# A recurrent layer and a feed-forward layer in one kernel: six weight tensors fetched ahead, the first products by token blocks, idle products in the front

## The chip, the cores and the metric

The kernel runs on one core of a Trainium2 chip. The metric is the device time of one execution in microseconds (us). The engines are named as the profile names them: PE is TensorE (matrix products; PEld is its loading of weights), DVE is VectorE, ACT is ScalarE, POOL is GpSimd, and SP is SyncE, which here only issues DMAs.

## The reference

Two layers follow each other. The first is a recurrence over 768 tokens in 4 batches of 8 heads, of head size 40; its output y, as 3072 rows of 320, goes through two matrix products with a softplus between them.

```python
    for t in range(S):
        kt, vt, qt = (k[:, :, t], v[:, :, t], q[:, :, t])
        m_new = np.maximum(f_gate[:, :, t] + m, i_gate[:, :, t])
        f_stab = np.exp(f_gate[:, :, t] + m - m_new)
        i_stab = np.exp(i_gate[:, :, t] - m_new)
        m = m_new
        C = f_stab[:, :, None, None] * C + i_stab[:, :, None, None] * np.einsum('bhd,bhe->bhde', vt, kt)
        n = f_stab[:, :, None] * n + i_stab[:, :, None] * kt
        h_tilde = np.einsum('bhde,bhe->bhd', C, qt)
        nq = np.einsum('bhd,bhd->bh', n, qt)[:, :, None]
        denom = np.maximum(np.abs(nq), 1.0)
        o = 1.0 / (1.0 + np.exp(-o_gate[:, :, t]))
        y[:, :, t] = o * h_tilde / denom
...
    h = x @ w_in
    g = np.maximum(h, 0.0) + np.log1p(np.exp(-np.abs(h)))
    return (g @ w_out).astype(np.float32)
```

Here x is y as 3072 rows of 320, w_in is 320 x 2048 and w_out 2048 x 320.

## The kernel before

The recurrence is computed in chunks of 128 tokens: 4 batches of 6 chunks are 24 steps, and three steps make one of 8 blocks of 384 tokens. Inside a chunk the recurrence becomes scores (sp), decays (pw) and products of the two with the values (yp). A tile x of 128 tokens by 320 is y, transposed on PE (xp) and cast by ACT into the high part of X; DVE subtracts to get its low part. X is what the second layer reads.

The second layer has 16 slices f of 128 of the 2048 hidden columns. For each block and slice PE makes hp from X with 8 products of 384 columns (wih and wil are the high and low parts of w_in, which the first engine mode needs to keep the precision), ACT makes the softplus gh, and PE adds gh times w_out to three banks po, one for each 128 tokens. In block 0 these last products use wof, the whole w_out in full precision; in later blocks its high and low parts woh and wol. The tiles hp lie in three buffers of PSUM (the tag hp), so a fourth slice waits until ACT has read the first.

The weights come as 16 tensors of 640 KB, wi0 to wi7 and wo0 to wo7, each holding two slices. They arrive as 64-bit words, and ACT (mag and sg, L218 to L233), POOL (some of the sg, L227) and DVE (L236) make 32-bit numbers of them in four instructions; then ACT casts the high parts (L260, L264 and L281) and DVE or POOL subtracts the low ones (L269, L271). Three of the raw tensors fit in the buffers at once (WB). This work, the next block's recurrence and the products run together through block 0.

The order of the instructions on each engine is fixed by in_order(): each follows the one written before it. What is written when is decided by tables. In the front, up to the first hp, the table F gives each event a number and the events run in the order of these numbers (in first_tile). Then products() counts the products of PE, and tick(n) runs every generator whose due count, from the tables Q, W, M, N, CI and CO, has been reached. Odd or even numbers of some entries of Q choose the engine (G: the conversion sg on POOL or ACT; H and J: the low parts on POOL or DVE).

Where ACT needs a function from another table of functions than the one loaded, a table load (ACT_TABLE_LOAD) stands in its order. In the front these are the sigmoids of the gates og and eg, the exponentials, and the softplus of gh.

later_gates() computes the gates of all chunks but the first: it reads the gate rows, takes exponentials, and scans; the results fz and fc go out to memory and come back spread over partitions (fb, fc).

Of the kernel before, what the change touches and what calls it, by code (L numbers as in the profile page):

```python
# [8 lines left out]
F32 = mybir.dt.float32  # L9
F32R = mybir.dt.float32r  # L10
# [34 lines left out]
def mlstm_moe_kernel(  # L45
# [113 lines left out]
    def later_gates():  # L159
# [3 lines left out]
        fs = p1.tile([NCHAIN, S], F32, tag="gb", name="fs")  # L163
        fg = fs[:, L:]
# [11 lines left out]
        nc.scalar.copy(fs[:, 0:L], fg0)  # L176
# [3 lines left out]
        fc = p1.tile([NCHAIN, S], F32, tag="gc", name="fc")  # L180
# [6 lines left out]
        nc.vector.tensor_tensor_scan(fc, fs, fc, 0.0, ALU.mult, ALU.add)  # L187
# [18 lines left out]
    woh = cpool.tile([128, NF, DM], F32R, name="woh")  # L206
# [67 lines left out]

    def weights_out(u, slope=False):
# [5 lines left out]
        nc.scalar.copy(woh[:, 2 * u : 2 * u + 2, :], wof[u])  # L281
# [13 lines left out]
    M = dict(FB=-23, LOAD=-50, Y=-9, SCAN=3, VI=-10, VW=10, IQ=25, SP=27, SPD=12, CN=33, CD=43, CE=49, CF=50, YQ=54,  # L295
             YQD=3, EV=47, YD=69, YD1=-30, RD=79, RY=-95, RZ=26, NM=116, FIN=128, XH=-9, XL=15)
    N = dict(FB=-26, LOAD=-57, Y=-7, SCAN=9, VI=-16, VW=22, IQ=23, SP=28, SPD=8, CN=30, CD=34, CE=39, CF=60, YQ=55,
             YQD=6, EV=17, YD=67, YD1=-32, RD=84, RY=-22, RZ=10, NM=125, FIN=150, XH=-9, XL=14)
    Q = dict(Gi0=68, Go0=50, Gi1=-42, Go1=1, Gi2=-47, Go2=36, Gi3=38, Go3=7, Gi4=6, Go4=18, Gi5=-8, Go5=31, Gi6=-10,
             Go6=7, Gi7=4, Go7=35, B3=40, B4=84, B5=125, B6=260, B7=300, B8=368, B9=446, B10=528, S0=-375, S1=-292,  # L300
             S2=-195, GT=-381, GL=52, LB=214, LS=33, SPD=-12, OF0=1, OF1=19, GR0=25, GR1=82, GR2=29, GR3=-26, GR4=18,
             GR5=38, LG=10, FS0=-51, FS1=25, FSW=-14, CI=-48, CO=-4, CS=34, K0=-23, K1=-29, CF=15, RC=-17, RS=92,
             B2=-20, B11=620, GT2=92, GL2=108, FS2=-31, GR6=-1, Hi0=-20, Ji0=63, Hi1=34, Ji1=78, Hi2=16, Ji2=34,
             Hi3=-12, Ji3=49, Hi4=-8, Ji4=-16, Hi5=36, Ji5=136, Hi6=-16, Ji6=107, Hi7=-67, Ji7=20)
    CI = dict(A=-6, B=2, C=-54, D=-2, E=10, F=30)
    CO = dict(A=3, B=-52, C=15, D=12, E=-36)
# [393 lines left out]
    def split_x(z):  # L700
# [3 lines left out]
        xp = work(z, ps_a, "pa", [128, 3, L], "xp", ps_h, "hp")  # L704
# [5 lines left out]
        nc.vector.tensor_tensor(X[:, 3:6, ts], xp, X[:, 0:3, ts], op=ALU.subtract)  # L710

# [3 lines left out]
    def first_tile(follow):  # L715
# [36 lines left out]
        for z in zs:  # L752
# [8 lines left out]
            fetch=fetch_next, fetch2=fetch_next, fetch3=fetch_next, wr=lambda: run(wparts),  # L761
        )
        for i, z in enumerate(follow):
            ev[f"lq{i}"] = lambda z=z: load(z)
            if i < 2:
                ev[f"lo{i}"] = lambda z=z: load_old(z)
# [154 lines left out]

    def products():
# [4 lines left out]
        def outs(po, t, f, put):  # L927
# [11 lines left out]
            else:  # L939
                terms = [(gh, woh[:, f]), (gh, wol[u][:, i]), (gl, woh[:, f])]  # L940
# [16 lines left out]
        for t in range(NT):  # L957
            po = []
            for f in range(NF):
                fsl = slice(f * 128, (f + 1) * 128)  # L960
                hp = ps_h.tile([128, T], F32, tag="hp", name=f"hp{t}_{f}")[:, 0 : SIZES[t] * L]
# [3 lines left out]
                X = Xs[t][:, :, 0 : SIZES[t] * L]  # L965
                seq = [
# [116 lines left out]
```

## Time and profile before

| | us |
|---|---|
| median of 3 runs | 462.56 |
| lowest and highest | 462.15, 462.60 |
| the profiled execution | 461.91 |
| its span on the chip | 460.2 |
| PE busy in the span | 433.4 |
| DVE, ACT, POOL busy | 303.9, 211.2, 137.2 |

The span is what the trace shows from the first instruction to the last; times below count from its start. The front lasts until the first hp product at 40.34, block 0 until about 105, and the blocks 1 to 7 fill the rest. The profile has a page with the busy time of the engines and other views: tables of busy time by stretch (with the granted clock of PE, where 1.00 is 2.4 GHz and 0.50 is 1.2 GHz), lists of what an engine waited for, and timelines of one engine, in which neighbouring instructions of one kind are one line. In a timeline a number in square brackets is the idle time before the line and who ended it.

### The profile page before, as it was taken

What the parts mean: (1) busy time and instruction counts of PE and PEld (TensorE: products, weight loads), DVE (VectorE), ACT (ScalarE), POOL (GpSimd) and SP (SyncE); (2) the same over time, 40 slices, a digit from 0 to 9 for tenths busy, and PEclk for the clock granted to TensorE, in tenths of its full rate; (3) what the DMA queues carried; (4) which work ended last, traced back from release to release, by engine and by line L of the source; (5) the groups of instructions that cost most, each with busy time, mean ns of one, the idle gap of its engine ahead of it and who ended that gap; (6) DMA issues with size and microseconds to landing.
All of it is one profiled execution on the core that took longest, in us unless ns stands there. A gap on an engine that the chain in (4) does not pass through costs nothing.

```text
span 460.2 us, 10555 instructions
## 1 busy us (share of the span) xinstructions
PE 433.4 (94%) x4266; PEld 402.9 (88%) x4266; DVE 303.9 (66%) x577; ACT 211.2 (46%) x416; POOL 137.2 (30%) x152
## 2 busy tenths in 40 slices
PE   5756799899999999999999999999999999999997
PEld 4555587677999999999999999999999999999996
DVE  4657488998987967766776867656876678242121
ACT  2727778784233642355333733463333543333332
POOL 8646078455531131233122312302223111000000
PEclk9975999999999999999999999999999999999999
DMA  7954967587656564654464263555374220101001
GB/s 200 333 188 115 274 197 246 147 214 168 178 180 182 154 151 122 164 144 96 150 185 117 74 204 108 129 143 138 105 196 129 78 78 19 41 0 46 0 1 43
DMA packets 38139, 62.55 MB, mean 136 GB/s; under 512 B 5626, under 2 KB 20258, under 8 KB 38090
## 3 DMA queue, kind: packets, MB, share of 16 engines
q1 hardware_dynamic: 25958, 53.62, 41.3%
q10 hardware_dynamic: 12132, 8.26, 6.3%
q8 instruction: 33, 0.54, 0.5%
q14 instruction: 16, 0.13, 0.1%
HBM read 53.60 MB, written 8.26 MB: 134 GB/s over the span
## 4 chain that ended last, share of the span: by engine, by line
PE 81%; DVE 9%; ACT 3%; POOL 3%; issue 2%; DMA 0%; SPq 0%; POOLq 0%; DVEq 0%; ACTq 0%
PE hp L978 36%; PE po L949 34%; PE yq L642 4%; PE sp L606 2%; PE sp L600 2%; POOL v L564 1%; DVE wof L236 1%; PE yp L619 1%; PE wm L723 1%; DVE wih L271 1%; PE fb L455 1%; DVE wil L269 1%; DVE mv L611 1%; DVE nm L685 1%; DVE gw L494 1%
## 5 line engine op out<-in xcount | busy, mean ns | idle before, releaser
L978 PE MATMUL hp<-X,wih 128*128 128x384 f32 x768 | 181.7, 344 | 4.0 <-ACT X L708 2.8
L978 PEld LDWEIGHTS hp<-X,wih 128*128 128x128 f32 x768 | 133.9, 189 | 9.0 <-ACT X L708 3.2
L854 ACT ACTIVATE gh<-hp 128x384 fp32r<-128x384 f32 x112 | 55.0, 491 | 181.8 <-PE hp L978 175.0
L858 DVE TENSOR_TENSOR gl<-hp,gh 128x384 fp32r<-128x384 f32 x112 | 61.6, 555 | 74.0 <-ACT hp L855 73.1
L949 PE MATMUL po<-wol,gh 128*128 128x320 f32 x336 | 71.2, 311 | 0.0
L949 PE MATMUL po<-woh,gl 128*128 128x320 f32 x336 | 70.3, 309 | 0.0
L949 PE MATMUL po<-woh,gh 128*128 128x320 f32 x336 | 69.8, 308 | 0.0
L978 PE MATMUL hp<-X,wil 128*128 128x384 f32 x256 | 66.6, 339 | 0.1
L500 POOL TENSOR_TENSOR vw<-vt,gw 128x328 f32<-128x328 f32 x23 | 21.7, 944 | 134.3 <-DVE gw L491 123.0
L564 POOL TENSOR_TENSOR v<-v,flast 40x328 f32<-40x328 f32 x37 | 38.2, 1032 | 69.4 <-DVE v L567 53.7
L949 PEld LDWEIGHTS po<-woh,gh 128*128 128x128 f32 x336 | 57.3, 188 | 0.1
L949 PEld LDWEIGHTS po<-woh,gl 128*128 128x128 f32 x336 | 54.9, 188 | 0.2
L949 PEld LDWEIGHTS po<-wol,gh 128*128 128x128 f32 x336 | 54.5, 188 | 0.5
L855 ACT ACTIVATE hp<-hp 128x384 f32<-128x384 f32 x112 | 54.5, 487 | 0.0
L978 PEld LDWEIGHTS hp<-X,wil 128*128 128x128 f32 x256 | 46.4, 189 | 0.9 <-DVE wil L269 0.5
L611 DVE TENSOR_TENSOR mv<-sp,pw 64x256 f32<-64x256 f32 x84 | 31.8, 417 | 14.7 <-PE sp L606 14.2
L482 POOL TENSOR_TENSOR v<-vt,gT 64x328 f32<-64x328 f32 x42 | 33.6, 801 | 22.5 <-DMA vt<-in_vko 19.6
L381 DVE TENSOR_TENSOR mv<-mv,fc 64x512 f32<-64x512 f32 (+1 forms) x42 | 39.1, 930 | 1.1 <-DMA fc<-fc_d 0.5
L949 PE MATMUL po<-wof,gh 128*128 128x320 f32 x96 | 28.5, 440 | 3.9 <-ACT v L544 2.7
L567 DVE TENSOR_TENSOR v<-v,sp 40x164 f32<-40x164 f32 x74 | 23.9, 323 | 12.0 <-POOL v L564 10.7
L439 DVE TENSOR_TENSOR_SCAN pw<-fb,near 128x512 f32<-128x512 f32 x21 | 26.4, 1255 | 3.8 <-DMA fb<-fz_d 3.8
L949 PEld LDWEIGHTS po<-wof,gh 128*128 128x128 f32 x96 | 17.6, 189 | 10.8 <-ACT v L544 3.0
(126 smaller groups left out, 439.9 us busy)
## 6 DMA issues: line engine op xcount, KB each, us to landing
qk<-in_qk SPq DMA_DIRECT2D x21, 416.0 KB
vt<-in_vko SPq DMA_DIRECT2D x23, 324.0 KB
fb<-fz_d SPq DMA_DIRECT2D x42, 128.0 KB
wi<-in_wts SPq DMA_DIRECT2D x8, 640.0 KB
wo<-in_wts SPq DMA_DIRECT2D x8, 640.0 KB
eg<-in_oT SPq DMA_DIRECT2D x7, 576.0 KB
out<-ob SPq DMA_DIRECT2D x24, 160.0 KB
yd<-y ACTq DMA_DIRECT2D x36, 96.0 KB
```

The costliest lines, as they stand in the source:

```text
L381: nc.vector.tensor_tensor(z.mv[ch][r], z.mv[ch][r], z.fc[r], op=ALU.mult)
L439: nc.vector.tensor_tensor_scan(pw.rearrange(flat), fb.rearrange(flat), eye.rearrange(flat), 0.0, ALU.mult, ALU.add)
L482: nc.gpsimd.tensor_tensor(vi, v1[r], g[r], op=ALU.mult)
L500: nc.gpsimd.tensor_tensor(z.vw, v1, z.gw.broadcast_to([128, H, E]), op=ALU.mult)
L564: nc.gpsimd.tensor_tensor(heads(whole), old, f, op=ALU.mult)
L567: nc.vector.tensor_tensor(dst[i], dst[i], z.cps[ch][dims(i)], op=ALU.add)
L611: nc.vector.tensor_tensor(half(z.mv[ch][r], i), sps[i][r], half(z.pw[r], i), op=ALU.mult)
L854: nc.scalar.activation(gh, hp, AF.Softplus)
L855: nc.scalar.activation(hp, hp, AF.Softplus)
L858: nc.vector.tensor_tensor(gl, hp, gh, op=ALU.subtract)
L949: nc.tensor.matmul(po[j], a[:, j * 128 : (j + 1) * 128], w, start=first, stop=(last and left[j] == 0))
L978: nc.tensor.matmul(hp, a, r, start=(i == 0), stop=(i == len(seq) - 1))
```

## The change

- Six weight tensors are loaded ahead. There are four raw buffers in place of three, and the fourth and fifth tensor (wi2 and wo1) go into buffers that will hold high parts of w_out later: woh, one tile before, becomes four tiles woh0 to woh3, and the two loads take the places of woh3 and woh2. On SP the five loads wi0, wi1, wo0, wi2, wo1 now stand in a row, and eg, qk and mv behind them.
- The eight products of the slices 0 and 1 of block 0 are made for each token block of 128 by itself, in the order blocks 1, 0, 2: 48 products of 128 columns in place of 16 of 384. They are events of the front now (h00 to h12), all behind the transposes and ahead of the third slice.
- keep_warm() puts products of the identity with itself, whose result wz nobody reads, into the front: 3 ahead of the first scores, 5 ahead of the second yp and 11 ahead of the last two xp.
- The tiles xp lie in the PSUM banks of po0, po1 and pa, not in those of hp.
- later_gates() holds the later gates apart from the first chunk's, without the copy of these (L176), scans in two parts and sends fz in two DMAs.
- The tables M, Q, CI, CO and F have new numbers. By them the third tile's scores go behind the first yp, the softplus table is loaded ahead of the eg sigmoids (o1s), the lows of wih of the tensors 2, 5 and 7 go from DVE to POOL, wil of 7 from POOL to DVE, and the conversions sg of wi6 and wo4 from ACT to POOL.

```diff
-        fs = p1.tile([NCHAIN, S], F32, tag="gb", name="fs")
-        fg = fs[:, L:]
+        fg = p1.tile([NCHAIN, w], F32, tag="gb", name="fg")
...
-        nc.scalar.copy(fs[:, 0:L], fg0)
...
-        nc.vector.tensor_copy(fc[:, 0:S:C], fs[:, 0:S:C])
-        nc.vector.memset(fs[:, 0:S:C], 0.0)
-        nc.sync.dma_start(fz_d.rearrange("c p s -> p c s"), fs.rearrange("p (c s) -> p c s", s=C))
+        parts = ((0, L, fg0), (L, S, fg))
+        for x, y, f in parts:
+            nc.vector.tensor_copy(fc[:, x:y:C], f[:, 0 : y - x : C])
+            nc.vector.memset(f[:, 0 : y - x : C], 0.0)
+            nc.sync.dma_start(fz_d[x // C : y // C].rearrange("c p s -> p c s"), f.rearrange("p (c s) -> p c s", s=C))
...
-    woh = cpool.tile([128, NF, DM], F32R, name="woh")
+    woh = [None] * (NF // 4)
...
-    WB, MB = 3, 2
+    WB, MB = 4, 2
+    STASH = (3, 4)
+    stashed = []
...
-        r = stage.tile([128, UW] + [2] * words, U32, tag="wr", bufs=WB, name=f"w{'io'[i]}{u}")
+        if words and len(raw) in STASH:
+            k = STASH.index(len(raw))
+            r = p1.tile([128, UW, 2], U32, tag=f"woh{3 - k}", name=f"w{'io'[i]}{u}")
+            stashed.append((6 - 2 * k, "io"[i] + str(u)))
+        else:
+            r = stage.tile([128, UW] + [2] * words, U32, tag="wr", bufs=WB, name=f"w{'io'[i]}{u}")
...
-        nc.scalar.copy(woh[:, 2 * u : 2 * u + 2, :], wof[u])
+        need(*[n for k, n in stashed if u >= k])
+        if u % 2 == 0:
+            woh[u // 2] = p1.tile([128, 4, DM], F32R, tag=f"woh{u // 2}", name=f"woh{u // 2}")
+        nc.scalar.copy(high(u), wof[u])
...
-    CI = dict(A=-6, B=2, C=-54, D=-2, E=10, F=30)
-    CO = dict(A=3, B=-52, C=15, D=12, E=-36)
+    CI = dict(A=-2, B=3, C=-81, D=9, E=0, F=30)
+    CO = dict(A=3, B=-76, C=15, D=8, E=-37)
...
-        xp = work(z, ps_a, "pa", [128, 3, L], "xp", ps_h, "hp")
+        xp = work(z, ps_a, "pa", [128, 3, L], "xp", *((ps_o, "po0"), (ps_o, "po1"), (ps_a, "pa"))[z.s])
...
+        def keep_warm(k):
+            n = max(0, Q[f"D{k}"])
+            if n and not idle:
+                idle.append(ps_h.tile([128, 4, 128], F32, tag="hp", name="wz"))
+            for i in range(n):
+                nc.tensor.matmul(idle[0][:, i % 4], ident, ident, start=True, stop=True)
...
+    def begin(f, g):
+        if f not in early:
+            early[f] = ps_h.tile([128, T], F32, tag="hp", name=f"hp0_{f}")
+        need(("X", g))
+        for _ in first_layer(early[f], 0, f, slice(g * L, (g + 1) * L)):
+            pass
...
-        zs = first_tile(rest[:3])
+        zs = first_tile(rest[:2])
```

first_layer() holds the eight products that stood in products(), for any range of tokens.

Three places show how the order moves. On PE, in the front: sp_0 are the scores of the third tile, sp_2 those of the second, yp_0_271 before and yp_0_267 after are the first attention product (the last numbers are the program's buffer numbers). Before:

```order
L585 MATMUL sp_0_0_261<-qk_0_144 128x128
L585 MATMUL sp_0_0_262<-qk_0_144 128x128
L619 MATMUL yp_0_271<-vi_0_221,pw_0_0_179 128x123 x4
L619 MATMUL yp_0_271<-vi_0_221,pw_0_1_181 128x123 x2
L619 MATMUL yp_0_271<-vi_0_221,pw_0_1_181 128x82
L619 MATMUL yp_0_271<-vi_0_221,pw_0_1_181 128x41
L619 MATMUL yp_0_288<-vi_0_233,pw_0_0_171 128x123 x4
```

After:

```order
L601 MATMUL sp_2_0_238<-qk_0_148 128x128
L601 MATMUL sp_2_0_239<-qk_0_148 128x128
L635 MATMUL yp_0_267<-vi_0_231,pw_0_0_168 128x123 x4
L635 MATMUL yp_0_267<-vi_0_231,pw_0_1_170 128x123 x2
L635 MATMUL yp_0_267<-vi_0_231,pw_0_1_170 128x82
L635 MATMUL yp_0_267<-vi_0_231,pw_0_1_170 128x41
L601 MATMUL sp_0_0_278<-qk_0_139 128x128
L601 MATMUL sp_0_0_279<-qk_0_139 128x128
```

The first yp stands directly behind the second tile's scores now, and the third tile's scores follow it.

On PE, from the last transposes to the first slices. Before:

```order
L619 MATMUL yp_0_328<-vi_0_257,pw_0_1_169 128x41
L706 MATMUL xp_0_355<-ident_79,x_0_352 128x128 x3
L706 MATMUL xp_0_369<-ident_79,x_0_349 128x128 x3
L978 MATMUL hp_0_407<-X_303,wih 128x384
L539 MATMUL cp_0_420<-vw_0_387,vt_0_152 40x41 x8
L978 MATMUL hp_0_407<-X_303,wih 128x384 x4
L978 MATMUL hp_0_407<-X_303,wil 128x384 x2
L978 MATMUL hp_0_407<-X_303,wih 128x384
```

After:

```order
L635 MATMUL yp_0_325<-vi_0_262,pw_0_1_166 128x41
L749 MATMUL wz<-ident_79 128x128 x11
L722 MATMUL xp_0_375<-ident_79,x_0_371 128x128 x3
L722 MATMUL xp_0_379<-ident_79,x_0_357 128x128 x3
L968 MATMUL hp_0_392<-X_320,wih 128x128 x5
L968 MATMUL hp_0_392<-X_320,wil 128x128 x2
L968 MATMUL hp_0_392<-X_320,wih 128x128 x6
L968 MATMUL hp_0_392<-X_320,wil 128x128 x2
L968 MATMUL hp_0_392<-X_320,wih 128x128 x6
```

Idle products stand ahead of the last two transposes, and the first slice begins with products of 128 columns, with no cp between.

On ACT, from X to the first activation (gh_0). Before:

```order
L708 CAST X_303<-xp_0_369 128x3x128
L738 ACTIVATE eg_251<-eg_251 128x1152
L738 ACTIVATE eg_367<-eg_367 128x1152
L748 ACT_TABLE_LOAD
L281 CAST woh<-wof_377 128x640
L220 ACTIVATE magi_409<-wi_359 128x640
L233 ACTIVATE sgi_411<-wi_359 128x640
L220 ACTIVATE mago_415<-wo_399 128x640
L233 ACTIVATE sgo_417<-wo_399 128x640
L544 COPY park<-cp_0_420 40x164 x2
L850 ACTIVATE gh_0_440<-hp_0_407 128x384
```

After:

```order
L774 ACT_TABLE_LOAD
L295 CAST woh_425<-wof_407 128x640
L764 ACT_TABLE_LOAD
L764 ACTIVATE eg_264<-eg_264 128x1152
L764 ACTIVATE eg_404<-eg_404 128x1152
L221 ACTIVATE magi_476<-wi_251 128x640
L234 ACTIVATE sgi_478<-wi_251 128x640
L221 ACTIVATE mago_482<-wo_253 128x640
L234 ACTIVATE sgo_484<-wo_253 128x640
L560 COPY park<-cp_0_487 40x164 x2
L880 ACT_TABLE_LOAD
L880 ACTIVATE gh_0_498<-hp_0_392 128x384
```

Where there was one table load ahead of woh there are three: one ahead of woh, one ahead of the sigmoids of eg, which moved behind woh, and one ahead of gh_0.

## Rows read from the trace of the kernel before

**Rows 1.** Page, busy time: engine, busy us, share of the span, instructions.
```profile
PE 433.4 (94%) x4266; PEld 402.9 (88%) x4266; DVE 303.9 (66%) x577; ACT 211.2 (46%) x416; POOL 137.2 (30%) x152
```

**Rows 2.** By stretch: length, busy PE, PEld, DVE, ACT, POOL, clock, DMA, GB/s.
```profile
21.80:25.10 3.30, 3.30 (x17) 3.30 (x17) 0.00 (x1) 0.00 (x0) 0.00 (x0) 0.50 1.00 232
29.90:35.80 5.90, 0.00 (x0) 0.00 (x1) 3.68 (x10) 1.60 (x3) 5.03 (x11) 0.68 0.33 112
32.00:45.60 13.60, 6.97 (x38) 5.36 (x38) 9.94 (x17) 8.59 (x13) 10.15 (x11) 0.50 0.46 138
36.90:48.00 11.10, 8.30 (x48) 6.96 (x47) 6.79 (x13) 10.96 (x17) 5.57 (x3) 0.61 0.61 160
45.70:75.90 30.20, 27.06 (x298) 22.00 (x298) 20.59 (x36) 23.08 (x46) 15.63 (x15) 1.00 0.78 232
75.90:105.20 29.30, 26.59 (x224) 19.95 (x224) 27.32 (x46) 22.77 (x40) 15.12 (x10) 1.00 0.70 197
```

**Rows 3.** What PE waited for from 20 to 106: total us, times, longest.
```profile
PE xp L706 <- DVE x L629: 6.6, 2, 6.0
PE hp L978 <- ACT X L708: 2.8, 1, 2.8
PE po L949 <- ACT v L544: 2.7, 1, 2.7
...
PE po L949 <- DVE wof L236: 1.2, 2, 1.0
```

**Rows 4.** Timeline of PE, front and first block: start, length, instructions, wait before.
```profile
19.91 1.75 PE L585 MATMUL sp<-qk 40*128 40x128 f32 x16 [2.60 <-DVE pw L574]
21.60 5.39 PE L619 MATMUL yp<-vi,pw 128*128 128x123 f32 x32
...
27.99 1.88 PE L619 MATMUL yp<-vi,pw 128*128 128x123 f32 x16
...
35.83 1.70 PE L706 MATMUL xp<-ident,x 128*128 128x128 f32 x6 [5.96 <-DVE x L629]
...
40.34 0.69 PE L978 MATMUL hp<-X,wih 128*128 128x384 f32 x1 [2.80 <-ACT X L708]
...
43.11 0.84 PE L978 MATMUL hp<-X,wil 128*128 128x384 f32 x2
...
46.56 1.21 PE L978 MATMUL hp<-X,wih 128*128 128x384 f32 x6
...
53.85 3.50 PE L949 MATMUL po<-wof,gh 128*128 128x320 f32 x12 [2.66 <-ACT v L544]
```

**Rows 5.** Timeline of DVE in the front.
```profile
31.55 0.17 DVE L623 TENSOR_SCALAR nq<-yp 128x8 f32<-128x8 f32 x1 [1.16 <-POOL og L626]
...
32.99 0.73 DVE L629 TENSOR_TENSOR x<-yp,og 128x320 f32<-128x320 f32 x1 [0.83 <-POOL og L626]
```

**Rows 6.** Timeline of ACT from X to the second woh.
```profile
36.93 0.48 ACT L708 CAST X<-xp 128x384 fp32r<-128x384 f32 x1 [5.43 <-PE xp L706]
...
42.42 1.28 ACT L748 ACT_TABLE_LOAD   x1
43.71 0.72 ACT L281 CAST woh<-wof 128x640 fp32r<-128x640 f32 x1
...
48.03 0.49 ACT L850 ACTIVATE gh<-hp 128x384 f32<-128x384 f32 x1
...
51.47 0.72 ACT L281 CAST woh<-wof 128x640 fp32r<-128x640 f32 x1 [1.74 <-DVE wof L236]
```

**Rows 7.** Timeline of DVE in the first block, early and late.
```profile
49.25 0.69 DVE L269 TENSOR_TENSOR wil<-sgi,wih 128x512 fp32r<-128x512 f32 x1 [2.46 <-ACT wih L260]
49.97 0.61 DVE L271 TENSOR_TENSOR wih<-sgi,wih 64x128 fp32r<-64x128 f32 x2
...
97.86 2.09 DVE L271 TENSOR_TENSOR wih<-sgi,wih 64x128 fp32r<-64x128 f32 x2
```

**Rows 8.** Timeline of POOL: a conversion.
```profile
39.42 2.40 POOL L227 TENSOR_SCALAR sgo<-wo 128x640 f32<-128x640 uint8 x1
```

More of the change, by code (lines that the diff above doesn't have):

```diff
@@ L273, in weights, with high @@
         yield
+    def high(u):
+        return woh[u // 2][:, 2 * u % 4 : 2 * u % 4 + 2, :]
     def weights_out(u, slope=False):
@@ L764, in first_tile @@
             ev[f"lq{i}"] = lambda z=z: load(z)
-            if i < 2:
-                ev[f"lo{i}"] = lambda z=z: load_old(z)
+            ev[f"lo{i}"] = lambda z=z: load_old(z)
+        for k in range(12):
+            ev[f"dz{k}"] = lambda k=k: keep_warm(k)
+        for f in range(2):
+            for g in range(SIZES[0]):
+                ev[f"h{f}{g}"] = lambda f=f, g=g: begin(f, g)
         for k in range(1, 7):
@@ L920, in mlstm_moe_kernel, with first_layer @@
     wparts = ahead()
+    early = {}
+    def first_layer(hp, t, f, ts):
+        X, fsl = Xs[t][:, :, ts], slice(f * 128, (f + 1) * 128)
+        seq = [
+            (wih[:, 0, fsl], X[:, 0]),
+            (wih[:, 1, fsl], X[:, 1]),
+            (wih[:, 2, fsl], X[:, 2]),
+            (wih[:, 0, fsl], X[:, 3]),
+            (wih[:, 1, fsl], X[:, 4]),
+            (wil[:, 0, fsl], X[:, 0]),
+            (wil[:, 1, fsl], X[:, 1]),
+            (wih[:, 2, fsl], X[:, 5]),
+        ]
+        for i, (a, r) in enumerate(seq):
+            need(("wih" if i in (0, 1, 3, 4) else "wi", f // 2))
+            nc.tensor.matmul(hp[:, ts], a, r, start=(i == 0), stop=(i == len(seq) - 1))
+            yield
+    def begin(f, g):
[4 more added lines that the diff above has]
+            pass
     def products():
@@ L959, in products @@
             for f in range(NF):
-                fsl = slice(f * 128, (f + 1) * 128)
-                hp = ps_h.tile([128, T], F32, tag="hp", name=f"hp{t}_{f}")[:, 0 : SIZES[t] * L]
+                ready = t == 0 and f in early
+                hp = early[f] if ready else ps_h.tile([128, T], F32, tag="hp", name=f"hp{t}_{f}")[:, 0 : SIZES[t] * L]
                 if f == 0:
@@ L964, in products @@
                         tick(queue[0][0])
-                X = Xs[t][:, :, 0 : SIZES[t] * L]
-                seq = [
-                    (wih[:, 0, fsl], X[:, 0]),
-                    (wih[:, 1, fsl], X[:, 1]),
-                    (wih[:, 2, fsl], X[:, 2]),
-                    (wih[:, 0, fsl], X[:, 3]),
-                    (wih[:, 1, fsl], X[:, 4]),
-                    (wil[:, 0, fsl], X[:, 0]),
-                    (wil[:, 1, fsl], X[:, 1]),
-                    (wih[:, 2, fsl], X[:, 5]),
-                ]
-                for i, (a, r) in enumerate(seq):
-                    need(("wih" if i in (0, 1, 3, 4) else "wi", f // 2))
-                    nc.tensor.matmul(hp, a, r, start=(i == 0), stop=(i == len(seq) - 1))
+                for _ in first_layer(hp, t, f, slice(0, SIZES[t] * L)) if not ready else range(8):
                     n += 1
```

51 lines of the change are left out of this document (28 added, 23 removed).

## The prediction

> **What bounds the kernel now.** The page's busy table comes first: TensorE is busy for 433.4 us of the 460.2 us span [rows 1], so there are 26.8 us to win without taking work from it. The table by stretches says where they lie. From 29.90 to 35.80 TensorE does nothing at all; in the 32.00 to 45.60 stretch its clock is 0.50, the lower level (1.2 GHz); from 45.70 to 75.90 it loses 3.14 us, of which 2.66 ahead of po; from 75.90 to 105.20 it loses 2.71 us [rows 2, 4]. Behind 105 its products stand in the same order before and after the change, so I leave that part alone. The list of what TensorE waits for between 20 and 106 us then gives names to the holes: 6.6 us for VectorE's x ahead of the transposes xp, 2.8 for ScalarE's cast of X ahead of the first hp product, 2.7 for ScalarE's copy v that frees the first po bank, and 1.2 for VectorE's wof [rows 3].
>
> Three waits make one chain. TensorE does the third attention product yp at 27.99 [rows 4], VectorE reaches that tile's nq at 31.55 and its x at 32.99 [rows 5], the last transposes start at 35.83 [rows 4], and ScalarE casts X at 36.93 [rows 6]. From there ScalarE has no hole: it is busy for 10.96 of the 11.10 us from 36.90 to 48.00 [rows 2], and gh0, the first activation, begins at 48.03, 11.10 us after the cast [rows 6]. It then waits 1.74 us for VectorE's wof ahead of woh at 51.47 [rows 6], and po starts at 53.85, 5.82 us after gh0 [rows 4]. So up to 53.85 the end is set first by VectorE, then by ScalarE; TensorE only follows. What the change is worth there is how much earlier po starts, less what TensorE then lacks.
>
> **The change part by part.** The sum is made against the profiled execution, 461.91 us, which is 0.65 below the median of the runs, 462.56; the forecast is moved to the median at the end.
>
> *Attention front.* The first yp no longer stands behind the 16 score instructions of the third tile (19.91, 1.75 us), so it can start near 19.95 in place of 21.60 [rows 4]. In before its 16 instructions ran at clock 0.50 (21.80 to 25.10) [rows 2]; a yp at full clock takes 1.88 with its run-out, 1.6 without (the 27.99 row) [rows 4]. TensorE then does three yp (4.8 to 5.6), the scores (1.75), six transposing instructions (about 0.6) and ten idle instructions. An idle product has 128 columns and two instructions; by the yp row (16 instructions, most of 123 columns, 1.88) one instruction is 0.12, so the five idle products cost 1.2 us and the eleven 2.6. The third yp ends at 19.95 + 8.3 to 9.2 = 28.3 to 29.1. VectorE has its nq a moment later, not at 31.55, because the conversion sgi, whose wil kept VectorE from the second tile's nq, now stands ahead of the first x. From that nq to the cast of X took 36.93 - 31.55 = 5.38 [rows 5, 6]; I keep that. The cast is at 33.7 to 34.6, taken 34.0, which is 2.9 us earlier. The eleven idle products lie in the hole ahead of the transposes (5.90 us with no work [rows 2]) and cost nothing; if x came 2 us sooner than I think they would be late by about that much.
>
> *ScalarE to gh0.* The same casts follow, but two loads of its table more: the preload for softplus now stands ahead of the two sigmoids of eg, so there is one load for softplus, one back to sigmoid, and one for softplus again ahead of gh0. One took 1.28 us at 42.42, and the next instruction began at 43.71, 0.01 behind its end [rows 6]. Nothing hides two more, since ScalarE had no hole there: +2.56. The copy of 0.28 us that falls away lies ahead of the chain and gives nothing. gh0 comes at 34.0 + 11.10 + 2.56 = 47.66, 0.4 before its old place. So the gain of the front is nearly eaten by ScalarE.
>
> *gh0 to po.* The lows of wih for the third pair of blocks move from VectorE to GpSimd, two instructions that took 0.61 us at 49.97 [rows 7], and wof comes that much earlier, within ScalarE's wait of 1.74 [rows 6]: 0.6 of the 5.82. po starts at 47.66 + 5.2 = 52.85, 1.0 us earlier.
>
> *First products by token blocks.* 48 products of 128 columns in place of 16 of 384. No row shows such a product. From above: what one of 384 columns takes, 1.21/6 = 0.20 at full clock and 0.84/2 = 0.42 at half [rows 4]; from below: a third of that, 0.07 and 0.14. That is 3.4 to 9.6 us at full clock, 6.7 to 20 at half. I take a third to a half, because the yp instructions of 123 columns at 0.12 stand between the bounds. They begin near 34, before the last X is cast, and have until the park copy ahead of gh0 (about 46) with the cp products behind them: at the value taken there is a cover of some 5 us and the term is nothing; at the upper bound at half clock they end at 54 and everything moves by 8 us.
>
> *The clock.* With that work done early, TensorE has again a hole: the third hp may run, the fourth needs the PSUM buffer that gh0 frees, so from about 41 to 47.7 there is nothing to do. In before a hole of that length (29.90 to 35.80) had the clock at 0.50 from 32.00 on, and it came back at 45.70, 5.3 us after the hp products had begun at 40.34 [rows 2, 4]. If it goes the same way the fourth hp and two cp run at half clock and it comes back near 53.3, so 0.5 us of po run at half: +0.3.
>
> *Block 0 after 76.* VectorE is busy for 27.32 of 29.30 us there [rows 2], and of TensorE's loss of 2.71 the 1.2 for wof is a wait for it [rows 3]. VectorE gives the lows of wih for two more pairs to GpSimd (one took 2.09 at 97.86, the other counts 0.61 as at 49.97) and takes one wil (0.69 at 49.25): 2.0 us less work [rows 7]. Against that, the wil of the sixth pair now stands behind mv and four more instructions, and wof of two pairs comes about 0.8 later. GpSimd takes two conversions of 2.40 [rows 8] and the lows, which delays its vw for the next steps. The ends are 2 gained and 1 lost; I take 0.3 gained, near the middle, since rows speak for both.
>
> *Loads.* Six weight tensors stand in a row in the DMA queue and two of them in woh's buffers; the DMA share was 0.33 from 29.90 to 35.80 [rows 2], so there was room. The gate scan sends its rows some 3 us earlier, but TensorE's first user of them is not among the waits of before [rows 3]. Both nothing. If the stashed tensors land late, ScalarE waits for them behind eg, and the gate of 36.90 to 48.00 gets longer one for one.
>
> Sum: -1.0 (po) + 0.3 (clock) - 0.3 (after 76) = -1.0, so 460.9 against 461.91, and 461.6 on the scale of the median.
>
> **The rivals.** *Slow clock under po.* The hole ahead of gh0 is as long as the one that cost the clock in before, and TensorE works only in pieces between gh0 and po. If it comes back 5.3 us after po has begun, not after the fourth hp, half of 5.3 is lost, 2.65 in place of 0.3: 461.6 + 2.35 = 464.0, slower. It decides once the clock returns more than about 2.6 us behind po's start. For it: the row from 32.00 [rows 2]. Against it: in before it held at 1.00 from 45.70 to 75.90, over the wait of 2.66 ahead of po [rows 2, 4].
>
> *The late waits go.* VectorE's two us less turn the 2.71 lost after 76 into 0.7, 2.0 won in place of 0.3: 461.6 - 1.7 = 459.9, faster. For it: VectorE is busy for 27.32 of the 29.30 us [rows 2]. Against: wof stands later in its row.
>
> *Dear table loads.* Each switch holds ScalarE for twice what the load row shows. Then two more cost 5.1, not 2.56: 461.6 + 2.6 = 464.2, slower. The row speaks against it, woh following 0.01 us after the load [rows 6]. The Trainium skill, page "ScalarE: Activation LUTs", section "What ACT_TABLE_LOAD costs", counts a drain of some 1.38 us with each load of 1.28, so 2.66 for every switch to another set; by that the two would be 5.3. This trace shows the load's 1.28 and no drain behind it.
>
> *The clock falls early, as before.* If it is at 0.50 from 21.80 to 25.10 again, half of those 3.3 us is lost: the cast of X is at 35.6, gh0 at 49.3, po at 54.5, 0.65 later than now, and the clock's +0.3 and block 0's -0.3 cancel: 463.2. For it: TensorE still waits for VectorE's first pw ahead of that point; against it: three idle products stand in that wait now.
>
> *Small products as dear as large ones*, the upper bound at half clock: 8 us more, about 469, slower.
>
> **How the numbers follow.** Forecast 0.40, slow clock 0.20, late waits gone 0.18, early fall 0.12, dear loads 0.07, small products 0.03. Each holds within about 1.0 us. 0.2% is 0.93 us, about what a measurement can tell from no change: faster is below 461.63, slower above 463.49. The forecast lies on the edge and gives 0.22 to faster and 0.18 to same; late waits gone give 0.18 to faster; the early fall 0.01, 0.07 and 0.04; slow clock 0.02 to same and 0.18 to slower; dear loads and small products 0.10 to slower. Together 0.41, 0.27 and 0.32. The range goes from 459.3 (just past the late waits) to 464.2 (past the slow clock and up to the dear loads); the forecast's own is 460.6 to 462.6.
>
> **What would show it.** X cast near 34.0, three table loads between it and gh0, gh0 near 47.7, po near 52.9, the clock back by 53.5, and TensorE's loss from 76 to 105 about as before. I am wrong in the front if the cast is not 2 us earlier; wrong on ScalarE if gh0 is more than 14 us behind the cast; wrong on the clock if po's first products run at 0.50 beyond 54; and wrong on block 0 if the loss after 76 differs by more than 1 us.

## The result

The changed kernel takes 465.49 us (median of 5 runs, 464.37 to 466.96) against 462.15 us of the kernel before beside it (5 runs, 461.36 to 462.6). The ratio is 1.0073, with a 95% interval from 1.0047 to 1.0099: 3.3 us slower where 1.0 us faster was forecast, and outside the range of 459.3 to 464.2. The profiled execution took 465.69 us, with a span of 464.0. Executions of one kernel differ here by up to 5.6 us, in eight of those of e11_both_wait_only by 4.2 us at one mean clock of 0.981, and four that took 483 to 843 us (two of the kernel before, two of e7_both_no_idle) are left out of the medians and ratios below.

Two marks divide the loss: the start of po, and the time from there to the end. po started at 53.85 in before [rows 4]; its span was 460.2, so 406.3 us followed. In the changed kernel it starts at 57.67, and 464.0 - 57.67 = 406.3 follow. All of the 3.8 us is lost ahead of po, and nothing is won or lost behind it.

The page of the changed kernel, busy time (as in [rows 1]):

```profile
PE 444.5 (96%) x4336; PEld 416.4 (90%) x4336; DVE 300.7 (65%) x575; ACT 213.0 (46%) x415; POOL 142.4 (31%) x159
```

TensorE is busy 11 us longer. The 19 idle products take some 6.0 us of this by their rows (0.83 at 14.19, below, 2.50 at 26.38 and 2.70 at 32.92), and TensorE works at half clock for longer. The busy time by stretch (length, busy time of the engines, granted clock, DMA), as in [rows 2]:

```profile
19.80:29.20 9.40, 8.37 (x45) 8.10 (x46) 6.74 (x17) 5.23 (x8) 2.93 (x5) 0.50 1.03 305
40.00:53.60 13.60, 13.60 (x75) 13.26 (x74) 5.35 (x14) 13.48 (x19) 4.14 (x3) 0.50 0.40 123
79.70:109.00 29.30, 26.33 (x225) 20.17 (x226) 26.41 (x45) 21.52 (x39) 21.40 (x15) 1.00 0.58 173
```

The first stretch, in which the scores and yp are done, stands at 0.50 throughout; in before only 21.80 to 25.10 did. So do the small products of the second. The third is block 0 behind 76, moved by the 3.8 us: 2.97 us lost there against 2.71. What TensorE waited for, as in [rows 3]:

```profile
PE yp L635 <- POOL vi L492: 3.8, 1, 3.8
PE xp L722 <- DVE x L645: 1.9, 1, 1.9
...
PE hp L968 <- DVE wil L277: 1.4, 1, 1.4
```

The 6.6 us for x have shrunk to 1.9, and the wait for X is gone, as the change meant it. Ahead of them is a new one of 3.8 us, put down to GpSimd's vi. The timeline of TensorE shows where it lies (as in [rows 4]):

```profile
14.19 0.83 PE L749 MATMUL wz<-ident 128*128 128x128 f32 x6
14.95 2.06 PE L601 MATMUL sp<-qk 40*128 40x128 f32 x32
20.83 3.61 PE L635 MATMUL yp<-vi,pw 128*128 128x123 f32 x16 [3.83 <-POOL vi L492]
...
40.53 1.48 PE L968 MATMUL hp<-X,wih 128*128 128x128 f32 x6
...
49.41 0.78 PE L555 MATMUL cp<-vw,vt 128*40 128x41 f32 x16
...
57.67 3.50 PE L1005 MATMUL po<-wof,gh 128*128 128x320 f32 x12 [1.62 <-ACT v L560]
```

The scores end at 17, the first yp starts at 20.83, and it takes 3.61 us where one at full clock took 1.88 [rows 4]. GpSimd, in the same stretch:

```profile
13.67 1.94 POOL L172 TENSOR_TENSOR ig<-ig,m 32x640 f32<-32x640 f32 x1 [1.42 <-DVE m L169]
15.58 2.99 POOL L476 TENSOR_SCALAR_AFFINE_SELECT pw<-pw 128x512 f32<-128x512 f32 x4
18.55 0.74 POOL L492 TENSOR_TENSOR vi<-v,gT 128x328 f32<-128x328 f32 x1
19.26 1.43 POOL L492 TENSOR_TENSOR vi<-vt,gT 128x328 f32<-128x328 f32 x2
```

VectorE:

```profile
11.92 1.67 DVE L169 TENSOR_TENSOR_SCAN m<-fg,m,ig 32x640 f32<-32x640 f32 x1 [6.98 <-DMA ig<-in_gates]
...
14.47 3.60 DVE L171 TENSOR_TENSOR fg<-fg,m 32x640 f32<-32x640 f32 x1
...
18.62 1.47 DVE L510 TENSOR_TENSOR gw<-gT,pw 128x4 f32<-128x4 f32 x3
20.01 1.27 DVE L590 TENSOR_TENSOR pw<-sp,pw 128x512 f32<-128x512 f32 x2
21.21 0.22 DVE L510 TENSOR_TENSOR gw<-gT,pw 128x4 f32<-128x4 f32 x2
```

The first yp needs the first vi, which ended at 19.29, and VectorE's first pw, which ran from 20.01 to 20.68. So it is pw that it waited for; the profile names vi because the third one, which this yp does not need, ended at about the same moment (in e2_two_loads_less, which leaves this order as it is, the profile names pw). And pw waited in its turn: VectorE's gw, three for 1.47 us at 18.62, are instructions of 128 x 4 numbers, of which two took 0.22 at 21.21. They stretch while GpSimd goes from one instruction to the next without a pause, and here pw starts at 20.01, while GpSimd's last vi still runs. The subtraction of 3.60 us at 14.47 lies in the same row. GpSimd's row begins with ig, and ig waits for VectorE's scan.

The scan waits until 11.92 for the rows of ig. The scan and that subtraction in the kernel before, and the issue of ig's rows on SP:

```profile
7.71 1.75 DVE L170 TENSOR_TENSOR_SCAN m<-fs,m,ig 32x640 f32<-32x640 f32 x1 [2.74 <-DMA ig<-in_gates]
...
10.60 1.14 DVE L172 TENSOR_TENSOR fs<-fs,m 32x640 f32<-32x640 f32 x1
```

```profile
3.90 0.42 SPq L166 DMA_DIRECT2D ig<-in_gates  x1
```

The same issue in the changed kernel:

```profile
4.29 0.35 SPq L444 DMA_DIRECT2D vt<-in_vko  x1
...
5.16 0.42 SPq L165 DMA_DIRECT2D ig<-in_gates  x1
```

The loads of the two gate rows were issued at 3.43 and 3.90 in before and are issued at 4.69 and 5.16 now, behind qk and vt of the third tile: 1.3 us later at the issue, 4.2 at the start of the scan, with the larger transfers ahead of them (two of 208 KB and one of 324, against rows of 80 KB). I did not cost this move.

ScalarE from the second of the three casts of X on, the one that I call the cast of X here as in the prediction (as in [rows 6]):

```profile
38.44 0.48 ACT L724 CAST X<-xp 128x384 fp32r<-128x384 f32 x1 [5.85 <-PE xp L722]
...
50.45 0.59 ACT L560 COPY park<-cp 40x164 f32<-40x164 f32 x2
51.05 1.28 ACT L880 ACT_TABLE_LOAD   x1
52.34 0.49 ACT L880 ACTIVATE gh<-hp 128x384 f32<-128x384 f32 x1
```

From the cast of X to gh0 are 13.9 us, as forecast (13.66), and from gh0 to po 5.33 (5.2). Only the cast itself is wrong: 38.44, not 34.0.

### The profile page after: what moved, and what is told of

Read it like the earlier page. It is cut to its first block, busy times and chain, and to the rows that moved or that the text cites. A ratio compares the mean times of both kernels' runs of the same rounds, so it can differ in the third digit from the quotient of the medians.

```text
span 464.0 us, 10700 instructions
## 1 busy us (share of the span) xinstructions
PE 444.5 (96%) x4336; PEld 416.4 (90%) x4336; DVE 300.7 (65%) x575; ACT 213.0 (46%) x415; POOL 142.4 (31%) x159
## 4 chain that ended last, share of the span: by engine, by line
PE 81%; DVE 4%; POOL 4%; ACT 4%; issue 2%; DMA 1%; SPq 0%; POOLq 0%
PE hp L968 36%; PE po L1005 35%; PE yq L658 4%; PE sp L622 2%; PE sp L616 2%; POOL v L580 1%; PE yp L635 1%; POOL sgo L228 1%; POOL sgi L228 1%; DMA fc<-fc_d 1%; DVE x L646 1%; POOL pw L476 1%; DVE mv L397 0%; DVE v L583 0%; POOL vi L492 0%
## 5 line engine op out<-in xcount | busy, mean ns | idle before, releaser
L968 PE MATMUL hp<-X,wih 128*128 128x384 f32 (+1 forms) x792 | 187.3, 347 | 0.5 <-ACT X L724 0.2
L968 PEld LDWEIGHTS hp<-X,wih 128*128 128x128 f32 x792 | 140.2, 195 | 4.4 <-ACT X L724 0.5
L968 PE MATMUL hp<-X,wil 128*128 128x384 f32 (+1 forms) x264 | 69.4, 343 | 1.4 <-DVE wil L277 1.4
L968 PEld LDWEIGHTS hp<-X,wil 128*128 128x128 f32 x264 | 49.1, 195 | 2.1 <-DVE wil L277 1.7
```

What stands on the lines that cost most here:

```text
L968: nc.tensor.matmul(hp[:, ts], a, r, start=(i == 0), stop=(i == len(seq) - 1))
```

## The experiments

Each changes one or two numbers of the tables or a few lines. The first four ran beside 21 executions of the kernel before (median 462.08 us), the next four beside 26 (462.50), the ninth to eleventh beside 22 (461.68), and the last beside 17 (461.54). These groups ran on different chips, the first and the last on one, so from one group to another the ratios to the kernel before are compared. A ratio is one of means, with its 95% interval, and can differ a little from that of the medians; each profile is of one execution.

**e1_gates_first.** The loads go back ahead of the third tile's qk and vt.

```diff
-lg0=138
+lg0=100
```

> The changed kernel with one thing undone: the two loads of the later gates stand ahead of the third tile's qk and vt again, as before the change. Theory (late gate rows): in the changed kernel the rows of ig landed at 11.8 us, in before at 7.6; VectorE's scan and GpSimd's ig and vi stand behind them, the first yp waits for vi until 20.8, and the clock falls in that wait. With the loads back the scan starts near 7.7, the first yp near 19.9, ScalarE casts the last X near 34 to 36 in place of 38.4, gh0 is still 13.9 behind it (the two loads of the table are kept), po near 53.5: 461 to 463 us. Rival (the front is late for another reason, the order on VectorE or the idle products): the cast of X stays near 38 and the time near 465.5.

Measured: 462.32 us, ratio to before 1.0013 [0.9985, 1.0040]. TensorE:

```profile
19.64 1.95 PE L635 MATMUL yp<-vi,pw 128*128 128x123 f32 x16 [1.96 <-DVE pw L590]
...
47.56 0.69 PE L968 MATMUL hp<-X,wih 128*128 128x384 f32 x1 [5.41 <-ACT gh L880]
...
52.34 5.36 PE L1005 MATMUL po<-wof,gh 128*128 128x320 f32 x12 [0.30 <-ACT v L560]
```

VectorE, the scan and the gw ahead of pw:

```profile
8.33 1.66 DVE L169 TENSOR_TENSOR_SCAN m<-fg,m,ig 32x640 f32<-32x640 f32 x1 [3.42 <-DMA ig<-in_gates]
...
14.83 4.07 DVE L510 TENSOR_TENSOR gw<-gT,pw 128x4 f32<-128x4 f32 x4 [1.44 <-POOL pw L476]
18.82 1.27 DVE L590 TENSOR_TENSOR pw<-sp,pw 128x512 f32<-128x512 f32 x2
```

GpSimd:

```profile
12.90 1.31 POOL L172 TENSOR_TENSOR ig<-ig,m 32x640 f32<-32x640 f32 x1
14.17 2.38 POOL L476 TENSOR_SCALAR_AFFINE_SELECT pw<-pw 128x512 f32<-128x512 f32 x4
```

ScalarE, and two stretches:

```profile
33.12 0.48 ACT L724 CAST X<-xp 128x384 fp32r<-128x384 f32 x1 [5.85 <-PE xp L722]
...
47.02 0.49 ACT L880 ACTIVATE gh<-hp 128x384 f32<-128x384 f32 x1
```

```profile
19.80:29.20 9.40, 9.40 (x91) 9.23 (x92) 6.68 (x20) 3.88 (x8) 3.39 (x5) 1.00 1.03 293
46.00:56.00 10.00, 8.13 (x47) 6.03 (x48) 5.46 (x7) 8.06 (x17) 5.14 (x7) 0.50 0.74 211
```

The scan starts at 8.33, GpSimd's row is done at 18.64 in place of 20.69 (four gw take 4.07 us until then), pw follows at 18.82, the first yp starts at 19.64 at full clock, the cast of X is at 33.12 and gh0 at 47.02, still 13.9 behind it. GpSimd's ig starts only 0.8 earlier than in the changed kernel (12.90 against 13.67), though the scan starts 3.6 earlier. The rest of the difference is in the row itself: in the changed kernel VectorE's addition and subtraction behind the late scan fall into it, and ig takes 1.94 there in place of 1.31, the four selects 2.99 in place of 2.38. That is the front as I had forecast it, and one number of the table separates it from the changed kernel. Of the 5.3 us that po comes earlier than in the changed kernel (52.34), the span gets 2.9: in this execution the clock is at 0.50 from 46 to 56, behind TensorE's wait of 5.4 us for gh0, and the 12 products of po take 5.36 in place of 3.50. 408.75 us follow po. This is what the rival of the slow clock under po had described.

**e2_two_loads_less.** Softplus is loaded behind the sigmoids of eg.

```diff
-tab=1147
+tab=1214
```

> The changed kernel with the softplus preload behind the two sigmoids of eg again, so that ScalarE loads its table once there and not three times; all else as it is. Theory (two loads on the path, but TensorE is next): in the changed kernel the small products and the cp behind them end at 50.2, and the park copy began at 50.45; without the loads ScalarE would be there at 49.2 and waits 1.0 us for cp, so gh0 comes at 50.8 in place of 52.3 and the time falls by 1.5, to 464.0. Rival (the loads alone set gh0): 2.56 less, 462.9. Rival (they are hidden): no change, 465.5.

Measured: 465.41 us, 1.0082 [1.0056, 1.0108], not to be told from the changed kernel; the 464.0 of the theory was missed. The profiled execution is the slowest of the six (467.16). TensorE:

```profile
21.77 3.61 PE L635 MATMUL yp<-vi,pw 128*128 128x123 f32 x16 [4.47 <-DVE pw L590]
```

ScalarE:

```profile
39.22 0.48 ACT L724 CAST X<-xp 128x384 fp32r<-128x384 f32 x1 [5.85 <-PE xp L722]
...
43.64 0.72 ACT L295 CAST woh<-wof 128x640 fp32r<-128x640 f32 x1 [0.89 <-DVE wof L237]
...
51.13 0.59 ACT L560 COPY park<-cp 40x164 f32<-40x164 f32 x2 [0.28 <-PE cp L555]
```

From X to gh0 are 12.5 us in place of 13.9, not 11.34: the loads had covered a wait of 0.89 us for wof, which the sigmoids covered in before, and the park copy now waits 0.28 for cp. Then po comes 6.37 us behind gh0 (58.10) in place of 5.33, since TensorE, at half clock, is still in the fourth slice. The two loads are 2.56 us on ScalarE and 0.4 at po.

**e3_both.** Both edits together.

```diff
-lg0=138
+lg0=100
-tab=1147
+tab=1214
```

> The changed kernel with both: gate loads first and two table loads less. Theory: the two losses are separate and nearly add; the cast of X at 34 to 36 and the park copy held by cp only if the small products run at half clock (10.3 us): gh0 at 46 to 48, po at 51.5 to 53, 458.5 to 461 us. Rival (the same wait, the clock, stands behind both): no better than the better of the two alone.

Measured: 461.17 us, 0.9996 [0.9964, 1.0028]. X is cast at 33.38, gh0 at 45.90, po at 52.12, and 407.3 us follow. By the medians the two edits give 4.3 us together, the first alone 3.2; the interval does not tell it from the kernel before. po comes 1.7 us earlier than in before [rows 4], and 1.0 of it is lost again behind po. That 1.0 is not the clock, which is at 1.00 from 51.5 on in this profile: at the start of block 1 TensorE waits for VectorE's part of X, a wait that the changed kernel does not have.

```profile
104.82 0.62 PE L968 MATMUL hp<-X,wih 128*128 128x384 f32 x2 [0.95 <-DVE X L714]
```

The profiles of e2_two_loads_less and e9_idle_in_wait have the same wait of 0.95, that of e1_gates_first one of 0.41, and that of e11_both_wait_only none; why is open.

**e4_before_two_loads_more.** The kernel before with the two table loads.

```diff
-tab=1012
+tab=960
```

> The kernel before with one thing added: its softplus preload stands ahead of the two sigmoids of eg, which puts two more table loads on ScalarE between the cast of X and gh0. Theory: ScalarE has no hole there, so gh0 comes 2.56 us later, at 50.6, po at 56.4, and the time is 462.2 + 2.6 = 464.8. Rival (each switch costs twice its row): 467.3. Rival (TensorE's work after gh0 hides part): under 463.5.

Measured: 465.53 us, 1.0092 [1.0055, 1.0128]. ScalarE:

```profile
36.54 0.48 ACT L708 CAST X<-xp 128x384 fp32r<-128x384 f32 x1 [5.44 <-PE xp L706]
...
50.35 0.49 ACT L850 ACTIVATE gh<-hp 128x384 f32<-128x384 f32 x1
```

gh0 comes 13.81 us behind the cast, not 11.10: 2.71 more, and po is 2.3 later than in before. A load takes 1.28 and no more follows it, so the rival of the dear loads falls. The median (of four) is 3.4 higher, 1.1 more than the price at po; in the profile the clock was low once more from 56.5 to 59.9, and 407.9 us follow po.

**e5_before_gates_late.** The kernel before with the gate loads behind qk and vt.

```diff
-lg0=139
+lg0=144
```

> The kernel before with one part of the change alone: the loads of the later gates' two rows stand behind the third tile's qk and vt. Theory (late gate rows): the rows land near 11.8 us in place of 7.6, VectorE's scan starts there, its gw and pw and GpSimd's vi come later, so the scores of the third tile ahead of the first yp wait for pw until about 21 in place of 19.9 and the cast of X comes 1 to 2 us later (36.93 before): 463 to 465 against 462.1. Rival (in the old order nothing of the front waits for them): no change.

Measured: 463.30 us, 1.0010 [0.9985, 1.0034]. In the profile, that of the slowest of the ten executions (465.08), the cast of X is at 38.12, 1.2 later, and po 1.2 later; the interval does not tell the time from that of the kernel before. In the old order the scores of the third tile stand between the wait and the first yp, and the low clock ended at 25.7. By these two kernels the late rows cost much only together with the new order.

**e6_both_whole.** e3_both with the first two slices as 16 large products: the events h00 to h12 do nothing.

```diff
-                ev[f"h{f}{g}"] = lambda f=f, g=g: begin(f, g)
+                ev[f"h{f}{g}"] = lambda f=f, g=g: None
```

> e3_both (gate loads first, two table loads less) with the first two slices of block 0 made as 16 products of 384 columns behind the last X, as before the change, and not as 48 of 128. Theory (the small products are dear): in e3_both one of 128 columns took 0.21 us at half clock, 48 of them 10.3 us, and the cp and the third slice behind them held ScalarE's park copy by 0.3 and TensorE into po; 16 of 0.32 are 5.1, the park copy no longer waits, po comes up to 1.2 us earlier: 460 against 461.2. Rival (the early start of the token blocks is worth more than their price): 1 us slower, 462. Rival: the clock alone decides, no difference that can be told.

Measured: 462.15 us, 1.0022 [0.9991, 1.0053]. The wait of the park copy is gone and gh0 to po is back at 5.34, as expected, but in this profile, of an execution 2.8 us above the median, the clock fell at 21 and again at 38 and 55, and 409.1 us follow po. Whether the token blocks are worth their price stays open here.

**e7_both_no_idle.** e3_both without the 19 idle products.

```diff
-            n = max(0, Q[f"D{k}"])
+            n = 0
```

> e3_both without the 19 idle products of the front. Theory (they keep the clock up): without them TensorE stands still some 4 us ahead of the last transposes, the clock is at 0.50 in the front in most runs, the cast of X comes later and the time rises by 1 to 2 us, to 462 or 463. Rival (they only take time): the second yp comes 1.2 us earlier and the cast of X near 32.5 in place of 33.4: 460.3. Rival: no difference.

Measured: 461.37 us (eight executions), 0.9977 [0.9955, 0.9998]. The clock was at 0.50 from 21.4 to 28.2 in the profile and X was cast at 35.63, where that of e3_both stood at 1.00 until 34: the clock does as the theory has it. But the time is not higher than that of e3_both: X comes 2.25 us later in the profile, po only 1.5, and 406.2 us follow it in place of 407.3.

**e8_gates_first_fill.** e1_gates_first with 16 idle products ahead of the third slice.

```diff
+                if t == 0 and f == 2:
+                    for i in range(16):
+                        nc.tensor.matmul(hp[:, 0:L], ident, ident, start=True, stop=True)
```

> e1_gates_first (gate loads first, three table loads kept) with 16 idle products more, ahead of the third slice of block 0, in the hole in which TensorE waits for gh0 (41.8 to 47.6 in e1_gates_first, behind which the clock was at 0.50 from 46 to 56 and po ran at half). Theory (that hole costs the clock): the hole shrinks to some 2 us, the clock stays up under po and the profile's time from po to the end falls from 408.8 to about 406.5: 460.3 against 462.3. Rival (the clock falls anyway, in the products ahead): the idle products take 6.9 us at half clock, the third slice and po come 2 to 4 us late: 464 to 466.

Measured: 465.01 us, 1.0058 [1.0034, 1.0082]: the rival. TensorE:

```profile
46.81 5.60 PE L1023 MATMUL hp<-ident 128*128 128x128 f32 x32
...
56.02 3.39 PE L1005 MATMUL po<-wof,gh 128*128 128x320 f32 x12
```

In this execution the clock fell in the small products already, at 36.9; the filling takes 5.6 us, the third and fourth slice come behind it, and po starts at 56.02, 7.2 us behind gh0.

**e9_idle_in_wait.** The changed kernel, gates late and three loads kept, with 16 idle products in the wait ahead of the first yp.

```diff
-D5=-16
+D5=16
```

> The changed kernel with its late gate loads and its three table loads, and 16 idle products more on TensorE, directly ahead of the first yp, in the wait of 3.8 us for vi (17.0 to 20.8). Theory (the wait does its harm by the clock): at full clock they take 3.5 us and end about where vi is done; the clock stays at 1.00 in the front, where it was 0.50 from 19.7 to 29.3, the first yp still starts near 20.8, the cast of X comes about 4 us earlier, at 34.5 in place of 38.4, and the time is 461 to 462.5. Rival (the late rows themselves cost it): the cast of X stays within 1 us of 38.4, 465.

Measured: 463.10 us (462.71 to 463.38), 1.0030 [1.0018, 1.0042]. TensorE, the first stretch, and the cast of X:

```profile
16.76 3.84 PE L749 MATMUL wz<-ident 128*128 128x128 f32 x32
21.51 1.95 PE L635 MATMUL yp<-vi,pw 128*128 128x123 f32 x16 [0.92 <-DVE pw L590]
```

```profile
19.80:29.20 9.40, 8.48 (x83) 8.15 (x81) 8.01 (x22) 5.86 (x10) 3.63 (x6) 1.00 1.04 298
```

```profile
34.99 0.48 ACT L724 CAST X<-xp 128x384 fp32r<-128x384 f32 x1 [5.85 <-PE xp L722]
```

The first yp starts later than in the changed kernel (21.51 against 20.83), but the clock is at 1.00 where it was 0.50, and X is cast 3.45 us earlier. po comes 3.4 earlier (54.24), and the time is 2.4 us less by the medians, 2.0 by the ratios (1.0030 against 1.0073). Of the 5.3 us between the casts of X in the changed kernel and in e1_gates_first, where the wait is short, 3.45 come back, although the first yp starts 0.7 later. So most of what the wait cost was the clock that it brought down, and the wait itself the lesser part.

**e10_both_idle_in_wait.** e3_both with 10 idle products at the same place.

```diff
-D5=-16
+D5=10
```

> e3_both (gate loads first, two table loads less) with 10 idle products more directly ahead of the first yp (2.2 us of a wait that was 2.6). Theory (in part of the runs of e3_both the clock still falls in that wait): the slow ones of its runs (463 to 465) go, the median is 460 against 461.2. Rival (the clock falls later in the front anyway): no difference that can be told.

Measured: 461.60 us, 0.9993 [0.9977, 1.0009]; no execution above 462.7, where e3_both had three above 463. So the long executions are gone, as expected, and the median is no lower.

**e11_both_wait_only.** The same without the five idle products ahead of the second yp.

```diff
-D3=5
+D3=0
```

> e10_both_idle_in_wait without the five idle products ahead of the second yp, which stand on the way to X. Theory: the second yp and the cast of X come 1.2 us earlier (32.2 in place of 33.4); ScalarE is then held by the cp behind the small products if these run at half clock, so 0 to 1.2 us less, 459 to 460. Rival (they hold the clock there): X at 34 or later and 461 or more.

Measured: 459.71 us, 0.9970 [0.9948, 0.9991]: faster than both kernels. Six of the eleven executions lie between 458.70 and 459.71, the others between 461.00 and 462.88. ScalarE:

```profile
32.58 0.48 ACT L724 CAST X<-xp 128x384 fp32r<-128x384 f32 x1 [6.18 <-PE xp L722]
...
36.97 0.72 ACT L295 CAST woh<-wof 128x640 fp32r<-128x640 f32 x1 [0.89 <-DVE wof L237]
...
44.49 0.59 ACT L560 COPY park<-cp 40x164 f32<-40x164 f32 x2 [0.32 <-PE cp L555]
```

X is cast at 32.58, 1.1 us ahead of e10_both_idle_in_wait. Then ScalarE waits 0.89 for wof and 0.32 for cp, and gh0 is at 45.09.

**e12_whole_cover.** e11_both_wait_only with the large first products of e6_both_whole, and the sigmoids ahead of woh.

```diff
-o1s=1213
-tab=1214
+o1s=1150
+tab=1151
...
-                ev[f"h{f}{g}"] = lambda f=f, g=g: begin(f, g)
+                ev[f"h{f}{g}"] = lambda f=f, g=g: None
```

> e11_both_wait_only (gate loads first, two table loads less, idle products in the wait ahead of the first yp, none ahead of the second) with two things more: the first two slices as 16 products of 384 columns behind the last X, and the sigmoids of eg ahead of the cast woh, where they cover its wait for wof (0.89 us in e11_both_wait_only). Theory (with the front mended ScalarE is held by that wait and by cp behind the small products, and TensorE enters po late by 0.6): X to gh0 falls from 12.5 to 11.2 us, gh0 to po from 5.9 to 5.3, po near 49.5, 458 us against 459.7. Rival (the first products, begun after the last X only, leave a hole in which the clock falls, as far as po): 460 to 462.

Measured: 460.70 us, 0.9976 [0.9954, 0.9998]. TensorE:

```profile
51.12 3.50 PE L1005 MATMUL po<-wof,gh 128*128 128x320 f32 x12 [0.86 <-ACT v L560]
```

X to gh0 is 11.21 and gh0 to po 5.33, as expected; but in this execution X was cast at 34.58, because GpSimd's row was done, and pw begun, 1.85 us later than in e11_both_wait_only (20.67 against 18.82) though the scan began no later, and the end is no earlier. That delay begins ahead of both edits, with TensorE's products fb of the first decays: they start at 9.97 behind a wait of 1.22 for GpSimd's pw, in e11_both_wait_only at 8.70 without one. The clock was low from 33.5 to 40.3 and from 47.1 to 50.6. The time lies in the rival's range and is not to be told from e11_both_wait_only; which of the two readings holds stays open.

## Why the prediction was wrong

*Attention front: wrong, and here the sum failed.* That the first yp "can start near 19.95" rested on the wait for pw that before showed, with all of its forerunners where they were. The change moves one of these, the gate rows, behind two transfers in SP's queue; my step on the loads named the weights, eg and the sending of fz, put them at nothing, and did not name this; nor does my list of the change, since the move is one number of the table F. With the rows late GpSimd's row of ig, selects and vi came late and took longer, VectorE's pw came late behind its gw, and the first yp waited until 20.83. The 0.9 us at the yp is the smaller part; the clock, taken as full, was half from 19.8 to 29.2, and the cast of X came 4.4 us behind my 34.0. e1_gates_first put the rows back and has the cast at 33.12; e9_idle_in_wait left them late, kept the clock up and has it at 34.99.

*The early fall of the clock* stood among the rivals, but with 3.3 us at half as in before and 0.12 of the chance; the row from 19.80 to 29.20 has 9.4 at half. The argument against it, three idle products in that wait, was wrong about the place: they stand ahead of the scores at 14.19, and the wait opened behind the scores.

*ScalarE to gh0: right in size* (13.9 against 13.66), and e4_before_two_loads_more shows the price of the two loads by itself, 2.71 at gh0. What I had not seen is that taking them out does not give it back (e2_two_loads_less): the waits for wof (0.89), for cp (0.28) and of po for TensorE's own products (1.04) take their place.

*gh0 to po: right*, 5.33 against 5.2.

*First products by token blocks: at the upper end of the estimate, with the cover mis-sized.* Six products of 128 columns took 1.48 us at half clock with their run-out, and 6 plus 2 of them 1.71 from start to start (40.10 to 41.81): 0.21 each, the upper end of what I took, 10.3 us for 48. They ended at 49.4 and the cp behind them at 50.2; ScalarE's park copy, which needs it, began at 50.45. The cover of some 5 us was in truth 0.3, since they ran at half clock throughout; in e1_gates_first, with the clock full there, the cp behind them ended at 40.1 and the park copy began at 45.13, a cover of 5.0. (The rival of the small products adds up to 469.6, not 469.)

*The clock ahead of po: wrong way, small effect.* I expected a hole from 41 to 47.7; with the small products begun at 39 and at half clock there was none, and the clock was back by 53.6, ahead of po. That this is near the forecast 53.3 is luck: the low stretch there was another one than I had described. The rival of the slow clock under po is true of the profile of e1_gates_first, where the hole exists, and not of the changed kernel.

*Block 0 after 76: right within its size.* 0.3 gained was expected, and the loss is 2.97 against 2.71, 0.3 more. The wait for the sixth pair's wil is there (1.4), as its later place in VectorE's order had it.

The sum by what was measured: +3.8 at po, 0 behind it, so 465.7 in the profiled execution. What stays open is why the clock falls in the first products in some executions (e3_both at 34.4, e8_gates_first_fill at 36.9) and only behind them in another with nearly the same front (e1_gates_first at 46), and what besides the clock makes the executions of one kernel differ.

## What to carry to other kernels

When a change moves DMA issues, cost the smallest transfers in the row as well: a small load that slips behind two large ones can land late by their transfers (4.2 us here), and what stands behind its user on each engine moves with it, on VectorE also what only waits for GpSimd to pause. A wait of TensorE cost more than its length here, since the clock came down with it; so price a new wait by both, and when a loss is larger than its wait, put idle products into the wait to see which part is the clock. And take a cost that is "on the path" as given back only up to the next wait behind it.

## What the runs showed of the hardware

- The clock of TensorE was at 0.50 from 19.8 to 29.2 behind an idle time of 3.8 us in the changed kernel, and at 1.00 over the same stretch when idle products filled that time (e9_idle_in_wait).
- VectorE's instructions with two inputs in SBUF took far longer while GpSimd ran without a pause. The first gw of e1_gates_first, 128 x 4 numbers, began at 14.83 and ended at 18.67, with GpSimd's last vi at 18.64; three more took 0.15 each behind it. The subtraction of 32 x 640 took 3.60 us in the changed kernel, from 14.47 to 18.08, inside GpSimd's row, and 1.14 in before. The Trainium skill has the rule: "SBUF — State Buffer", section "SBUF: two separate sides", says that VectorE, with two such inputs, and GpSimd share a pair of ports of which one holds the whole for an instruction. The traces agree, and show besides that with GpSimd's instructions back to back VectorE can be without a turn for 3.8 us (e1_gates_first). It does get one at times: in the changed kernel the subtraction ended inside the row, in the longest of the selects (1.23 us, the others 0.63). By that rule a late row of GpSimd could have been seen to reach pw.
- A product of 128 columns with high and low parts took 0.21 us at half clock, where one of 384 took 0.32 (two of them from 52.55 to 53.19 in the changed kernel): a third of the columns for two thirds of the time.
